# Gated linear attention and a feed-forward block: the same steps in another order on all engines, and the PSUM banks given out anew

## The chip, the cores and the metric

One core of one Trainium2 chip runs the whole kernel in one launch. The metric is the device time of one execution in microseconds (us). TensorE is PE in the profile, its weight loads PEld, VectorE is DVE, ScalarE ACT, GpSimd POOL, and SP is the engine that here issues all DMAs.

## The reference

Two blocks follow each other. The first is a gated linear recurrence for 4 batches, 8 heads, 768 tokens and 48 numbers a head:

```python
for t in range(S):
    state = alpha[:, :, t, :, None] * state + np.einsum('bhd,bhe->bhde', k[:, :, t], v[:, :, t])
    y[:, :, t] = np.einsum('bhd,bhde->bhe', q[:, :, t], state)
```

Its output, put together as x of 3072 tokens by 384, goes through a feed-forward block with 2048 inner features:

```python
h = x @ w_in
g = h * np.clip(h + 3.0, 0.0, 6.0) / 6.0
out = g @ w_out
```

[...]

## The kernel before

**Tiling.** Tokens are taken in 24 chunks j of 128, six to a batch, and the feed-forward block works on 12 groups g of two chunks. All matmuls are in 32-bit floats; each shows as two records in the trace.

**Steps.** The kernel is a list of some 1,790 words such as `M.6.5` or `m.15`. Each word names a step, and behind the dots stand its chunk or group, its part, and for steps that write PSUM or a shared buffer the number of the bank or buffer. The steps of the attention, for chunk j:

- `la`, `lk`, `lq`, `lv` load alpha, k, q, v (SP), `w` loads a slice of weights (SP, 768 KB). `d1`, `d2`, `dx` (ACT), `d3` (DVE) and `d4` (POOL) convert a slice.
- `ta`, `tk`, `tq` turn alpha, k and q: PE transposes into PSUM for the first six chunks (L282), DVE transposes after that. `ca` places alpha (ACT, later DVE); `r` and `p` are its two running products (DVE scans); `k` and `q` scale by them (DVE).
- `sc` are the scores of two halves of a chunk (PE, L346), `m` masks them into the tile A (DVE, four instructions of 0.41 us, L356), `qa` places q below them in A (ACT, L366).
- `kb` and `ck` turn k back by PE and ACT; from chunk 8 on `kt` (DVE), `kw` and `kr` (SP) do it through DRAM.
- `u` multiplies k by v (PE, L429), `sm` adds that to the state (DVE, L437 and L439), `st` decays the state (POOL, L409) and `sv` places it among the rows of v (ACT, L419).
- `ya` and `yb` multiply A by v and the placed state (PE, L455), `cy` copies the result out as x (ACT, L464).

The steps of the feed-forward block, for group g: group 0 and 1 use plain products `f`, `fa`, `fb` (PE, L478, L489) with `fr` (ACT) and `fg` (DVE) for the activation, and group 0's second product is `b`, `bo`, `so`. From group 2 on the first product is done by a scheme of 20 smaller products `M` of 8 matmul records each (L600): `x`, `y` and `xc` make the sums that it needs (DVE, L537, L541, L647), `n` copies a product out (ACT, L606), `o` combines (DVE), `e` and `h` are the activation (ACT L494, DVE L498). The second product is done from group 1 on by 7 products `P` of 16 records each (L703), with sums `s` (DVE, L647), copies `K` (ACT), sums `G` (DVE, L719; ACT for the last of four) and stores `O` (SP). `z.m.n` issues n filler matmuls into bank m, whose results nothing reads (L532).

**Order.** No scheduler reorders anything. `run` calls the steps of the list from left to right, each appends its instructions to the queues of its engines, and an engine goes through its queue in that order:

```python
for word in words.split():
    name, *at = word.split(".")
    steps[name](*(int(x) for x in at))
```

So the list fixes the order on every engine, and which step waits for which follows from the data and from the buffers. PSUM has eight banks: four (`banks`, number 0 to 3) for transposes, scores, `u` and `ya`, and four (`bank_m`) for the products of the feed-forward block and the fillers. A step that writes a bank waits until the last step that read it is done.

**Pads.** Chunks from 6 on are loaded in blocks into one of two buffers each for alpha, k and q. Six memsets (L257, POOL) fill the ends of such a buffer; they are part of `load_akq` for the first use of each buffer, that is in la, lk and lq of chunks 6 and 7.

Of the kernel before, what the change touches and what calls it, by code (L numbers as in the profile page):

```python
# [17 lines left out]
def kernel(  # L18
# [228 lines left out]

    def load_akq(name, j):
        src = rows({"a": alpha, "k": k, "q": q}[name], j)
        if j < FIRST:  # L250
            nc.sync.dma_start(out=ring[name, j % NR][:, :, 0:D],
                              in_=src.rearrange("h s d -> s h d"))
            return
        to = quads[name, j % NQ]
        if j < FIRST + NQ:
            for o in (BLK, 3 * BLK):
                nc.gpsimd.memset(to[o : o + BLK, :, V - 1, D - BLK : BLK], 1.0)  # L257
        to = to.rearrange("r p v d -> r p (v d)")
        t = src.rearrange("(p a) (u v) d -> a u p (v d)", a=2, v=V)
        for o in range(4):  # L260
            skip = BLK * (o % 2)
            nc.sync.dma_start(out=to[BLK * o : BLK * (o + 1), :, 0 : V * D - skip],
                              in_=t[o // 2, :, :, skip : V * D])
# [457 lines left out]
    def store2(g, i):  # L721
# [8 lines left out]
        "lq": lambda j: load_akq("q", j), "lv": load_v, "w": load_weight,  # L730
# [14 lines left out]
    def run(words):  # L745
        for word in words.split():
            name, *at = word.split(".")
            steps[name](*(int(x) for x in at))

    with tc.manual_schedule():  # L750
        run("""z.0.5 z.0.3 z.0.1 z.0.8 qa.0.0 w.0 d2.0 d3.0 la.0 ta.0.0 ca.0 r.0 lk.0 tk.0.1 k.0
               z.0.2 p.0 la.1 ta.1.2 lq.0 tq.0.3 ca.1 r.1 lk.1 lv.0.0 sv.0.0 d1.0 kb.0.0 ck.0 z.0.2
               u.0.2.1 sm.0.0 sv.0.1 q.0 qa.0.1 tk.1.0 k.1 p.1 z.0.2 sc.0.2.3 m.0 la.2 ta.2.0 ca.2
               dx.0 w.2 d2.2 kb.1.0 ck.1 lq.1 r.2 sm.0.1 st.1 tq.1.2 q.1 d3.2 z.0.3 d1.2 dx.2 lv.1.1
               u.1.3.1 sv.1.0 sm.1.0 p.2 sm.1.1 sc.1.0.2 m.1 ya.0.3 yb.0 cy.0 lq.2 w.1 d1.1 tq.2.1
               q.2 d4.2 lk.2 tk.2.3 k.2 fa.2.0 d4.0 st.2 sc.2.0.2 d2.1 d3.1 m.2 dx.1 d4.1 qa.1.1
               lk.3 la.3 ta.3.1 ca.3 la.4 fa.0.1 sv.1.1 w.3 r.3 ta.4.3 ca.4 r.4 tk.3.1 k.3 kb.2.0
               qa.1.0 d2.3 ya.1.2 yb.1 cy.1 fa.1.2 lq.3 ck.2 d1.3 p.3 d3.3 lv.2.2 u.2.3.2 sm.2.0
               d4.3 fb.2 tq.3.1 q.3 fb.1 qa.2.0 sm.2.1 sv.2.0 st.3 fr.0.2.0 fg.0.2 lk.4 tk.4.0
               sv.2.1 w.5 d2.5 k.4 d3.5 d1.5 qa.3.0 d4.5 qa.2.1 sc.3.1.3 m.3 w.6 d2.6 d1.6 d3.6 d4.6  # L760
               lv.3.0 lq.4 w.7 kb.3.2 fb.0 f.0.3.3 kb.4.0 ya.2.1 ck.3 u.3.3.2 sm.3.0 fr.0.3.1 fg.0.3
               fr.0.1.0 fg.0.1 qa.3.1 sv.3.0 sm.3.1 p.4 d2.7 sv.3.1 d1.7 d3.7 d4.7 f.0.5.0 fr.0.5.1
               fr.0.0.0 fg.0.5 fg.0.0 tq.4.3 ck.4 la.5 ta.5.2 f.0.6.3 ca.5 w.4 d2.4 ya.3.0 yb.3 cy.3
               fr.0.6.1 yb.2 cy.2 w.9 d2.9 q.4 qa.4.1 d1.4 d1.9 dx.4 la.6 w.8 d3.4 r.5 lk.5 w.10
               d3.9 p.5 ca.6 fg.0.6 d4.9 w.12 lq.5 lv.4.1 d2.8 d3.8 f.0.7.2 d1.8 st.4 d4.8 d4.4 w.11
               fr.0.7.0 fg.0.7 f.1.7.0 fr.1.7.1 fg.1.7 sc.4.0.2 m.4 f.1.1.1 fr.1.1.0 fg.1.1 f.1.3.3
               fr.1.3.1 d2.10 d1.10 tk.5.3 f.1.0.2 d2.12 d3.10 d4.10 w.13 fg.1.3 fr.1.0.0 fg.1.0 k.5
               d3.12 lq.6 f.1.6.0 f.1.2.1 u.4.1.0 sm.4.0 d1.12 d4.12 sv.4.0 qa.4.0 ya.4.2 fr.1.6.1
               fg.1.6 w.15 tq.5.3 fa.4.3 sv.4.1 d2.11 kb.5.1 d2.13 fr.1.2.0 f.1.4.2 fr.1.4.1 d1.11
               sm.4.1 q.5 r.6 d3.11 d3.13 fg.1.4 d4.11 lv.5.0 lk.6 tq.6 p.6 d2.15 d3.15 fg.1.2 d1.13  # L770
               d4.13 sc.5.0.3 yb.4 f.1.5.0 fr.1.5.1 fg.1.5 tk.6 m.5 b.1.0.2 fb.4 b.1.1 d1.15 d4.15
               st.5 y.5 w.14 la.7 lk.7 cy.4 d2.14 qa.5.1 ck.5 b.0.0.1 fr.0.4.0 d3.14 k.6 q.6 ca.7
               fg.0.4 d1.14 d4.14 x.0 y.1 y.10 b.0.1 y.0 y.2 u.5.2 P.1.0.0 K.1.0 qa.5.0 sv.5.0
               qa.6.1 P.1.1.3 b.0.2 b.1.2 kb.6.0 ya.5.3 y.6 s.1.0.0 sm.5.0 sv.5.1 G.1.0.0 tk.7
               s.1.1.1 s.1.2.3 x.1 yb.5 cy.5 b.1.3 sc.6.1.2 lv.6.2 ck.6 u.6.3.0 s.1.3.2 x.2 P.1.2
               b.0.3 K.1.1 y.7 s.1.4 s.1.5 y.11 y.3 r.7 xc.2.1 x.3 y.4 y.8 xc.2.3 k.7 xc.2.0 xc.2.4
               y.9 y.12 y.16 y.13 y.15 P.1.3.3 K.1.2 P.1.4 bo.1 P.1.5 xc.2.5 G.1.1.1 P.1.6 y.14 y.17
               y.19 xc.2.6 sm.6.0 G.1.2.2 y.20 M.2.0.2 lv.12.1 la.8 O.1.1 O.1.0 ca.8 y.18 y.21 y.23
               so.1 G.1.3.3 n.2.0.8 bo.0 lq.7 lv.7.0 O.1.2 m.6 xc.2.2 xc.2.10 xc.2.7 tq.7 r.8 p.7
               xc.2.8 sv.6.1 M.2.15.3 M.2.1 kb.7.3 n.2.1.9 M.2.16 M.2.2 n.2.2.10 M.2.7.0 n.2.7.11  # L780
               sm.6.1 xc.2.9 q.7 p.8 M.2.3 M.2.4 n.2.4.12 M.2.8 o.2.0.0 M.2.5 n.2.5.13 qa.7.0 sv.6.0
               st.7 lk.8 O.1.3 lq.8 lk.9 la.9 la.10 tk.8 tq.8 lq.10 lq.9 ya.6.1 yb.6 M.2.9 z.1.3
               M.2.18.1 o.2.1.0 e.2.1.1 M.2.10 cy.6 ck.7 sc.7.0.2 u.7.1.3 n.2.10.14 M.2.11 qa.7.1
               ca.9 la.11 y.22 M.2.6.2 h.2.1 q.8 m.7 e.2.0.0 h.2.0 n.2.11.15 qa.6.0 n.2.18.10 qa.8.1
               M.2.12 M.2.19 n.2.12.12 M.2.13 sm.7.0 sv.7.1 r.9 k.8 o.2.3.0 sv.7.0 ya.7.0 y.24
               o.2.5.0 n.2.13.12 o.2.2.0 yb.7 cy.7 sc.8.1.2 xc.3.1 o.2.2.1 e.2.2.1 xc.3.3 o.2.3.1
               M.2.14 xc.3.4 xc.3.0 xc.3.5 o.2.4.0 xc.3.7 xc.3.6 o.2.6.0 P.2.0.1 M.3.0.2 M.2.17
               h.2.2 o.2.6.1 e.2.3.0 h.2.3 o.2.7.0 K.2.0 n.3.0.12 M.3.1 n.3.1.9 e.2.5.1 M.3.7.0
               n.3.7.13 xc.3.8 o.2.7.1 xc.3.2 kt.8 e.2.6.0 h.2.6 tk.9 M.3.2 n.3.2.10 e.2.4.0 P.2.1.3
               h.2.4 h.2.5 s.2.0.14 e.2.7.0 G.2.0.1 h.2.7 M.3.3 M.3.4 n.3.4.8 k.9 s.2.1.11 M.3.8  # L790
               o.3.0.0 ca.10 kt.9 P.2.3.3 s.2.2.15 s.2.3.14 lv.8.2 kw.8 kr.8 lk.10 sm.7.1 xc.3.9
               M.3.5 n.3.5.11 K.2.2 e.3.0.1 xc.3.10 M.3.9 o.3.1.0 P.2.2 K.2.1 u.8.0.3 M.3.18.2 s.2.5
               M.3.10 n.3.10.14 n.3.18.15 e.3.1.0 s.2.4 P.2.4 tq.9 h.3.0 st.8 sv.8.0 M.3.11 n.3.11.8
               tk.10 p.9 sm.8.0 q.9 r.10 k.10 qa.9.0 qa.9.1 m.8 sm.8.1 h.3.1 M.3.19 o.3.5.0 kt.10
               P.2.5 G.2.2.0 st.9 M.3.12 sc.9.0.1 qa.8.0 n.3.12.10 o.3.3.0 kw.9 lv.9.0 kr.9 sv.8.1
               u.9.2.3 sm.9.0 sv.9.1 sv.9.0 G.2.1.2 sm.9.1 st.10 M.3.15.2 M.3.16 M.3.6.3 M.3.13 m.9
               o.3.4.0 o.3.6.0 tq.10 n.3.13.10 o.3.2.0 e.3.4.1 ya.8.2 yb.8 ya.9.3 yb.9 cy.9 M.3.14
               M.3.17 cy.8 xc.4.1 P.2.6 e.3.5.0 G.2.3.3 o.3.2.1 xc.4.3 h.3.4 xc.4.4 o.3.6.1 xc.4.5
               xc.4.0 xc.4.6 e.3.2.1 M.4.0.0 n.4.0.10 P.3.0.1 xc.4.7 o.3.7.0 p.10 h.3.5 o.3.3.1
               xc.4.8 M.4.7.3 M.4.1 xc.4.2 h.3.2 o.3.7.1 lk.11 O.2.2 tk.11 e.3.6.0 e.3.3.1 h.3.3  # L800
               P.3.1.2 e.3.7.1 n.4.1.13 M.4.2 K.3.0 ca.11 q.10 h.3.6 r.11 k.11 h.3.7 n.4.7.15
               lv.10.2 lv.11.0 kw.10 sc.10.0.1 kr.10 G.3.0.0 u.10.3.2 sm.10.0 qa.10.1 n.4.2.14 M.4.3
               M.4.4 M.4.8 s.3.0.9 xc.4.9 s.3.2.12 s.3.1.11 P.3.3.2 n.4.4.8 M.4.5 o.4.0.0 e.4.0.0
               sv.10.1 sm.10.1 xc.4.10 kt.11 O.2.0 O.2.3 lq.11 m.10 s.3.3.9 s.3.5 M.4.9 o.4.1.0
               P.3.2 sv.10.0 st.11 n.4.5.11 K.3.2 la.13 M.4.18.0 p.11 tq.11 lk.12 tk.12 K.3.1 M.4.10
               n.4.10.9 q.11 qa.10.0 n.4.18.12 e.4.1.1 la.12 s.3.4 ca.12 h.4.0 r.12 P.3.5 G.3.2.1
               h.4.1 M.4.11 P.3.4 n.4.11.8 M.4.12 n.4.12.14 qa.11.0 M.4.19 p.12 G.3.1.3 lq.12 kw.11
               O.2.1 tq.12 kr.11 u.11.3 sc.11.0.2 sv.11.0 O.3.1 lk.13 P.3.6 qa.11.1 M.4.6.2 G.3.3.2
               k.12 o.4.3.0 m.11 sm.11.0 sv.11.1 kt.12 M.4.13 n.4.13.14 q.12 o.4.3.1 e.4.3.0 o.4.2.0
               o.4.6.0 h.4.3 o.4.2.1 ya.10.1 ya.11.0 yb.10 yb.11 cy.11 cy.10 xc.5.1 ca.13 xc.5.3  # L810
               M.4.15.1 M.4.16 M.4.14 P.4.0.2 o.4.4.0 M.4.17 xc.5.4 o.4.5.0 xc.5.0 xc.5.5 M.5.0.0
# [121 lines left out]
```

## Time and profile before

| | |
|---|---|
| time, median of 3 runs | 533.5 us (533.48 to 533.62) |
| the profiled execution's own time | 533.84 us |
| its span in the profile | 531.8 us, so 2.0 us lie around it |
| TensorE's granted clock over the span | 1.00 |
| busy: PE, DVE, ACT, POOL | 522.2, 477.0, 257.4, 50.4 us |
| M products (L600), 1,600 records | 82.8 + 52.5 + 42.0 + 31.8 us in four groups |
| P products (L703), 1,232 records | 121.7 + 91.5 us in two groups |
| filler matmuls (L532), 58 records | 10.2 us |
| pads (L257), 12 memsets on POOL | 0.9 + 0.8 + 0.6 us |

The span runs from the first to the last instruction or transfer of the execution. Busy time is the time in which at least one instruction of an engine was running; PE's matmuls overlap each other, so the sum of the groups' means is larger than the busy time. In the view of 40 slices one slice is 13.3 us and a digit is the busy share in tenths. "A <- B" in a view of waits reads: the step A stood idle until B was done.

### The profile page before, as it was taken

To read this page: it belongs to the slowest core of one execution; us is meant where nothing else is said; L and a number is where in the kernel's file an instruction comes from. 1 tells how busy PE (TensorE), PEld (TensorE's weight loads), DVE (VectorE), ACT (ScalarE), POOL (GpSimd) and SP (SyncE) were. 2 spreads that over 40 slices of the span, in tenths; PEclk is the share of its full clock that TensorE was granted. 3 is DMA by queue.
4 is the path that set the end of the run, shared out by engine and by line. 5 is a ranking of instruction groups with operands and counts; after the bars stand their busy time and mean duration, and the time that the engine had idled before them with its cause. 6 is when DMAs were issued, how large, how long until landed. Compare 5 with 4: busy or idle time off the path is not lost.

```text
span 531.8 us, 15143 instructions
## 1 busy us (share of the span) xinstructions
PE 522.2 (98%) x6306; PEld 496.9 (93%) x6306; DVE 477.0 (90%) x849; ACT 257.4 (48%) x503; POOL 50.4 (9%) x71
## 2 busy tenths in 40 slices
PE   7799999999999999999999999999999999999997
PEld 7698886789999999999999999999999999999997
DVE  6999989999999999999999999999999899496382
ACT  3889865212653553553544444642634544553340
POOL 5333425100000000000000000000000000000000
PEclk9999999999999999999999999999999999999999
DMA  9998887006615156254345356055364052100001
GB/s 173 218 254 247 211 231 156 18 2 149 155 31 118 30 125 139 49 137 100 89 107 118 90 123 143 18 134 111 92 138 105 10 110 44 44 2 2 15 16 37
DMA packets 124100, 54.40 MB, mean 102 GB/s; under 512 B 83328, under 2 KB 116864, under 8 KB 124032
## 3 DMA queue, kind: packets, MB, share of 16 engines
q1 hardware_dynamic: 124032, 53.44, 44.0%
q8 instruction: 49, 0.80, 0.7%
q14 instruction: 19, 0.16, 0.1%
HBM read 44.50 MB, written 8.91 MB: 100 GB/s over the span
## 4 chain that ended last, share of the span: by engine, by line
PE 81%; DVE 9%; ACT 3%; DMA 3%; POOL 2%; issue 1%; SPq 0%; DVEq 0%; POOLq 0%; ACTq 0%
PE m_ps L703 34%; PE m_ps L600 34%; PE m_ps L478 4%; PE t_ps L455 3%; PE t_ps L346 2%; PE t_ps L429 2%; DMA v<-in_v_dram 1%; DMA raw<-in_moe_w_out_dram 1%; DVE rings L647 1%; DVE R L309 1%; DVE raw L537 1%; ACT raw L186 1%; DVE g_sb L647 1%; ACT raw L191 1%; DVE w L537 1%
## 5 line engine op out<-in xcount | busy, mean ns | idle before, releaser
L606 ACT COPY g_sb<-m_ps 128x512 f32<-128x512 f32 x110 | 63.6, 584 | 123.7 <-PE m_ps L600 104.3
L703 PE MATMUL m_ps<-w,g_sb 128*128 128x192 f32 x704 | 121.7, 327 | 0.0
L703 PEld LDWEIGHTS m_ps<-w,g_sb 128*128 128x128 f32 x704 | 113.7, 190 | 0.4
L703 PE MATMUL m_ps<-rings,g_sb 128*128 128x192 f32 x528 | 91.5, 326 | 0.0
L703 PEld LDWEIGHTS m_ps<-rings,g_sb 128*128 128x128 f32 x528 | 85.4, 190 | 0.1
L600 PE MATMUL m_ps<-xc,w 128*128 128x128 f32 x640 | 82.8, 277 | 0.4 <-DVE w L541 0.4
L600 PEld LDWEIGHTS m_ps<-xc,w 128*128 128x128 f32 x640 | 77.5, 192 | 1.7 <-issue 0.6
L494 ACT ACTIVATE r<-g_sb,half 128x512 f32<-128x512 f32 x80 | 56.8, 722 | 33.1 <-DVE g_sb L541 12.1
L498 DVE SCALAR_TENSOR_TENSOR g_sb<-r,g_sb 128x512 f32<-128x512 f32 x80 | 53.7, 683 | 4.3 <-ACT r L494 3.9
L600 PE MATMUL m_ps<-xT,raw 128*128 128x128 f32 x400 | 52.5, 277 | 0.0
L600 PEld LDWEIGHTS m_ps<-xT,raw 128*128 128x128 f32 x400 | 48.6, 192 | 0.6
L409 POOL TENSOR_TENSOR st<-sm,R 128x192 f32<-128x192 f32 x20 | 12.9, 643 | 352.2 <-DVE sm L439 305.5
L647 DVE TENSOR_TENSOR g_sb<-g_sb 128x512 f32<-128x512 f32 (+1 forms) x55 | 41.9, 792 | 0.2
L600 PE MATMUL m_ps<-xT,w 128*128 128x128 f32 x320 | 42.0, 276 | 0.0
L600 PEld LDWEIGHTS m_ps<-xT,w 128*128 128x128 f32 x320 | 39.3, 192 | 0.1
L366 ACT COPY A<-q 48x256 f32<-48x256 f32 x88 | 35.6, 404 | 5.0 <-DVE q L332 3.8
L356 DVE TENSOR_TENSOR A<-t_ps,mask 64x256 f32<-64x256 f32 x96 | 36.0, 413 | 0.4
L478 PE MATMUL m_ps<-xT,w 128*128 128x256 f32 x144 | 32.8, 382 | 0.1
L600 PE MATMUL m_ps<-xc,raw 128*128 128x128 f32 x240 | 31.8, 276 | 0.0
L309 DVE TENSOR_TENSOR_SCAN R<-t,ones 128x516 f32<-128x516 f32 x24 | 29.6, 1235 | 1.0 <-ACT t L300 0.9
L478 PEld LDWEIGHTS m_ps<-xT,w 128*128 128x128 f32 x144 | 26.7, 190 | 3.8 <-POOL w L217 0.2
L600 PEld LDWEIGHTS m_ps<-xc,raw 128*128 128x128 f32 x240 | 29.6, 192 | 0.1
(104 smaller groups left out, 725.8 us busy)
## 6 DMA issues: line engine op xcount, KB each, us to landing
raw<-in_moe_w_out_dram SPq DMA_DIRECT2D x8, 768.0 KB, 5.3
raw<-in_moe_w_in_dram SPq DMA_DIRECT2D x6, 768.0 KB, 6.6
v<-in_v_dram SPq DMA_DIRECT2D x48, 96.0 KB, 3.1
out_dram<-oh SPq DMA_DIRECT2D x44, 96.0 KB, 1.7
far<-kq SPq DMA_DIRECT2D x64, 64.0 KB, 2.2
kb<-far SPq DMA_DIRECT2D x64, 64.0 KB, 2.1
aq<-in_alpha_dram SPq DMA_DIRECT2D x36, 96.0 KB, 2.7
qq<-in_q_dram SPq DMA_DIRECT2D x36, 96.0 KB, 2.5
```

The costliest lines, as they stand in the source:

```text
L309: nc.vector.tensor_tensor_scan(out=reverse(R, n - 1, n), data0=reverse(ax, n, n), data1=reverse(ones, n, n), initial=0.0, op0=ALU.mult, op ...
L356: nc.vector.tensor_tensor(out=to[:, a], in0=sc[a][half], in1=mask[half, half].unsqueeze(1).to_broadcast([HB, NP, HB]), op=ALU.mult)
L366: nc.scalar.copy(out=to[:, a], in_=Q_t[j][64 * a : 64 * a + D, :, half])
L409: nc.gpsimd.tensor_tensor(out=st, in0=sm, in1=R_t[j][:, :, 0:1].to_broadcast([C, NP, D]), op=ALU.mult)
L455: nc.tensor.matmul(y_of(j, (i + 1) // 2, p)[:, HB * b : HB * b + HB], vb[:, p, e : e + 32], A_t[j][:, b, 2 * p + a], start=(b == 0 and i = ...
L478: nc.tensor.matmul(h[:, f], w1[:, kk, o : o + C], xT_t[g][:, kk], start=(kk == 0), stop=(kk == KT - 1))
L494: nc.scalar.activation(out=to, in_=h, func=AF.Relu, bias=half, scale=1.0 / 6.0)
L498: nc.vector.scalar_tensor_tensor(out=to, in0=r, scalar=1.0, in1=h, op0=ALU.min, op1=ALU.mult)
L600: nc.tensor.matmul(acc[g][i][:, f * C : (f + 1) * C], spots[w][:, f * C : (f + 1) * C], x_of(g, x), start=(first and f == 0), stop=last, s ...
L606: nc.scalar.copy(out=slots[z], in_=acc[g][i])
L647: nc.vector.tensor_tensor(out=out, in0=in0, in1=in1, op=ALU.subtract)
L703: nc.tensor.matmul(to[g], a, rhs[:, f], start=(first and f == 0), stop=(last and f == HF - 1), skip_group_check=True)
```

## The change

**A new step.** The memsets leave `load_akq` and become a step of their own, `pd`, one word for each of the two sets of buffers:

```diff
+    def pad(r):
+        for name in "akq":
+            for o in (BLK, 3 * BLK):
+                nc.gpsimd.memset(quads[name, r][o : o + BLK, :, V - 1, D - BLK : BLK], 1.0)
+
     def load_akq(name, j):
...
         to = quads[name, j % NQ]
-        if j < FIRST + NQ:
-            for o in (BLK, 3 * BLK):
-                nc.gpsimd.memset(to[o : o + BLK, :, V - 1, D - BLK : BLK], 1.0)
...
-        "lq": lambda j: load_akq("q", j), "lv": load_v, "w": load_weight,
+        "lq": lambda j: load_akq("q", j), "lv": load_v, "pd": pad, "w": load_weight,
```

**A new list.** All words are put into another order, so every engine's queue changes. Apart from the bank numbers the words are the same, but for `pd.0` and `pd.1`, which come in, and four words `qa.0.0`, `qa.6.0`, `qa.12.0` and `qa.18.0`, which issued nothing and go. The number of filler matmuls stays 29, of which 13 instead of 17 stand ahead of the first transpose. The start of the list:

```diff
-        run("""z.0.5 z.0.3 z.0.1 z.0.8 qa.0.0 w.0 d2.0 d3.0 la.0 ta.0.0 ca.0 r.0 lk.0 tk.0.1 k.0
-               z.0.2 p.0 la.1 ta.1.2 lq.0 tq.0.3 ca.1 r.1 lk.1 lv.0.0 sv.0.0 d1.0 kb.0.0 ck.0 z.0.2
-               u.0.2.1 sm.0.0 sv.0.1 q.0 qa.0.1 tk.1.0 k.1 p.1 z.0.2 sc.0.2.3 m.0 la.2 ta.2.0 ca.2
-               dx.0 w.2 d2.2 kb.1.0 ck.1 lq.1 r.2 sm.0.1 st.1 tq.1.2 q.1 d3.2 z.0.3 d1.2 dx.2 lv.1.1
...
+        run("""w.0 z.0.5 la.0 lq.0 lk.0 z.1.8 la.1 d2.0 lv.0.0 d1.0 d3.0 pd.0 ta.0.0 z.1.1 lk.1
+               ca.0 sv.0.0 tq.0.1 dx.0 r.0 la.2 pd.1 z.1.3 w.2 tk.0.0 p.0 z.1.2 lq.1 ta.1.2 k.0
+               d4.0 z.1.2 ca.1 lv.1.1 q.0 kb.0.3 z.1.2 ck.0 sc.0.1.2 lq.2 r.1 qa.0.1 u.0.3.0 z.1.3
+               sm.0.0 z.0.3 m.0 sv.0.1 ya.0.3 w.1 yb.0 sm.0.1 d2.2 p.1 la.3 tk.1.0 ta.2.2 cy.0 lk.2
```

The stretch around chunk 15:

```diff
-               n.6.18.10 K.5.1 P.5.5 G.5.2.3 r.16 k.16 e.6.0.0 h.6.0 h.6.1 o.6.6.0 M.6.19 n.6.10.15
-               o.6.5.0 M.6.11 tq.16 P.5.4 qa.15.1 sc.15.1.2 m.15 u.15.0.3 n.6.11.12 sv.14.0 sv.14.1
-               st.15 sv.15.0 sm.15.0 M.6.12 n.6.12.14 o.6.3.0 sm.15.1 kt.16 G.5.1.1 p.16 M.6.15.3
-               M.6.16 M.6.13 n.6.13.14 o.6.4.0 ca.17 o.6.2.0 ya.15.1 ya.14.2 yb.14 sv.15.1 yb.15
...
+               P.5.5 K.5.1 sm.14.0 lq.18 ca.16 sv.14.1 sm.14.1 r.16 la.18 M.6.9 st.15 u.15.2.0 k.16
+               sv.15.0 sc.15.1.3 o.6.1.0 P.5.4 sm.15.0 e.6.1.1 p.16 sv.15.1 sm.15.1 kt.16 st.16
+               M.6.10 kw.16 q.16 G.5.1.1 m.15 M.6.5 n.6.10.15 ya.15.0 n.6.5.11 yb.15 r.17 lk.18
```

**Banks.** 151 words write another bank than before, among them 35 `M`, 23 `u`, 22 `P`, 20 `sc` and 14 `ya`; `ya.15.1` above, for example, becomes `ya.15.0`, and `sc.15.1.2` becomes `sc.15.1.3`. Lines behind the new function stand two lower in the changed kernel's profile.

## The prediction

> **What bounds the kernel now.** I read the busy table and the 40 slices first, then the stretches by stage, then the waits of TensorE (PE) and of VectorE (DVE), then the timeline around one late hand-over. The page first:
>
> ```profile
> PE 522.2 (98%) x6306; PEld 496.9 (93%) x6306; DVE 477.0 (90%) x849; ACT 257.4 (48%) x503; POOL 50.4 (9%) x71
> PE   7799999999999999999999999999999999999997
> DVE  6999989999999999999999999999999899496382
> ACT  3889865212653553553544444642634544553340
> DMA  9998887006615156254345356055364052100001
> ```
>
> PE is full from the third slice on, but DVE is nearly as full until slice 31 of 40, and the DMA rings are full in the first seven. So an order that delays DVE a little can delay PE. By stretches (busy us of each engine, then clock, DMA share, GB/s):
>
> ```profile
> 0.00:13.30 13.30, 10.58 (x64) 9.72 (x64) 8.62 (x17) 4.76 (x6) 7.12 (x20) 1.00 1.12 173
> 13.30:26.60 13.30, 9.99 (x243) 8.30 (x246) 12.89 (x26) 11.72 (x16) 4.28 (x3) 1.00 1.08 218
> 40.00:60.00 20.00, 19.92 (x276) 16.99 (x275) 19.56 (x31) 19.59 (x34) 7.51 (x7) 1.00 0.77 232
> 60.00:80.00 20.00, 20.00 (x222) 17.33 (x221) 18.38 (x32) 13.56 (x22) 7.30 (x8) 1.00 0.86 225
> 200.00:250.00 50.00, 50.00 (x595) 49.37 (x586) 47.52 (x87) 22.09 (x46) 0.51 (x1) 1.00 0.45 102
> 450.00:500.00 50.00, 50.00 (x526) 49.50 (x525) 30.80 (x60) 20.19 (x41) 0.00 (x0) 1.00 0.07 16
> ```
>
> PE loses 6 us in the first 26.6 us and almost nothing later; DVE has 2.5 us to spare in 200 to 250 us and plenty after 450. The waits after 32 us, of PE (first line, the only one) and of DVE from 130 to 400 us (the three largest):
>
> ```profile
> PE m_ps L600 <- DVE w L541: 0.4, 1, 0.4
> DVE g_sb L537 <- PE m_ps L600: 2.1, 3, 1.2
> DVE g_sb L498 <- ACT r L494: 1.3, 3, 0.6
> DVE xc L537 <- ACT xT L464: 1.0, 1, 1.0
> ```
>
> In the middle it is DVE that waits for PE, never the other way round after 128 us. One place shows the spare time, the mask of chunk 15 (m.15, L356) in front of its attention product (ya.15, L455):
>
> ```profile
> 301.82 1.95 PE L600 MATMUL m_ps<-xT,raw 128*128 128x128 f32 x16
> 301.87 0.77 DVE L356 TENSOR_TENSOR A<-t_ps,mask 64x256 f32<-64x256 f32 x2
> 303.60 1.06 PE L600 MATMUL m_ps<-xc,raw 128*128 128x128 f32 x8
> ```
>
> The last two of m.15's four mask instructions end at 302.64, ya.15 starts on PE at 304.59: 1.95 us spare.
>
> **How I count.** For each engine I add what lies ahead of a step in its list, start to start: PE 0.893 us for an M (8 records of 0.112), 2.60 for a P (16 of 0.163), about 0.4 to 0.5 for a transpose, score or attention word, 0.1 more at a change from big to small products; DVE the mean of the row less the 82 ns by which its instructions overlap, and 117 ns more where one waits for the instruction right before it. A step's lag is its start in the trace less that sum. PE's lag is 1.5 us at its first filler, 12.0 at 32 us, 14.5 at 147 us, 16.2 at ya.15, 18.0 at the last product (526.2). DVE's is 8.8 at m.2 (27.9 us), 14.3 at 144 us, 19.7 at m.15; from 144 us on it grows by waiting for PE, as the rows above show.
>
> **The change, part by part.**
>
> *Work.* The same instructions run, but for four words that issued nothing. PE's sum is 510.8 us before and 510.3 after (43 instead of 46 changes from big to small products): **-0.5**. DVE's is 468 in both. Waits on the instruction just before go from 82 to 84 on DVE, 0.2 us, taken at nothing. The last store's chain (P.11.6, an eviction on ACT, a store) is the same: 0.
>
> *Pads.* Twelve memsets (L257, 0.9 + 0.8 + 0.6 = 2.3 us in all on POOL) leave the loads of chunks 6 and 7 and run early as pd.0 and pd.1, around the state copy sv.0.0 and ahead of POOL's first weight conversion d4.0. POOL is at 7.12 of 13.3 us there, waiting for d3. Price for d4.0 between 0 and 2.3 us; it reaches only fa.0's weights, which come after the transposes, and I take 0. Behind the old place (47 to 84 us) nothing waited for POOL: no gain.
>
> *Front.* 13 filler matmuls (z, two records each) instead of 17 stand ahead of the first transpose ta.0. In the trace filler records start 213 ns apart until 6.96 us and 111 ns apart from then on; 26 records from 1.47 end at about 7.0, just behind alpha's landing (6.93), so ta.0 can start at about 7.1 instead of 7.97: -0.9. A rule of the Trainium skill speaks against this edit: "TensorE: Matmul & The Clock Gate", Part 1, has the clock open only after some 3.4 us of sustained work, in a window that runs freely, so the number of slow matmuls differs from run to run; were it to open later, ta.0 would run slow. By the two spacings ta.0's eight records would then cost 8 x 0.10 = 0.8 us more, and the sum below would be 0.8 higher at worst. This trace opened the clock 5.5 us after the first filler, and I take the same point. Of the 0.9 little is left on DVE: the new SP order brings q's first chunk before k's, so lk.0 and la.1 land about 1.2 us later (loads of this size land that far apart here: la.0 6.93, lk.0 8.16, lq.0, two later, 10.55), and lk.2 about 0.8 later. Adding up to m.2 I get an end at 29.2 to 29.6 against 29.42: DVE is where it was. PE gains more. In the old order DVE's sum up to q and ACT's copy for ya.1 was 3.9 us longer than PE's sum ahead of ya.1; in the new one the worst such place of the first 30 us (m.2 ahead of ta.4) is 1.9. PE's lag at 32 us comes out 1.5 to 2 lower: about **10 to 10.5**.
>
> *Middle.* Here the new order spends what the front gives. Covers are PE's sum ahead of the consumer less DVE's sum up to the end of the producer; PE's lag has to be at least DVE's lag less the cover.
>
> m.7 to sc.8: 132.8 - 129.2 = +3.5 before; 129.6 - 131.2 = -1.6 after.
> m.11 to ya.11: 210.0 - 207.0 = +2.9; 204.8 - 207.8 = -3.1.
> m.15 to ya.15: 288.4 - 282.8 = +5.5; 281.7 - 285.8 = -4.2.
> G.7.1 to P.7.6: 368.0 - 356.9 = +11.0; 360.4 - 364.1 = -3.8.
>
> (0.1 us of hand-over is in each.) The new order puts 3 us more of DVE's work ahead of m.15 and takes 7 us of PE's work away from before ya.15. If DVE is at m.15 with the lag of 14.3 that it had at 144 us, and loses nothing more, m.15 ends at 285.8 + 14.3 = 300.1 and ya.15 starts at 300.2, with a PE lag of 18.5, against 16.2 before: **+2.3**. DVE's lag at that place is bounded by 12.3 (8.8 as at m.2, and 3.5 of the 5.5 us that it lost from 28 to 144 us) and by 17 (14.3 and half of the 5.4 us of waits of 144 to 301 us): PE lag 16.5 to 21.2, that is +0.3 to +5.0. I take 14.3, since the new front leaves m.2 where it was, ACT is as full in 40 to 60 us (19.59 of 20 us), and DVE's waits for PE mostly go when PE is the late one. DVE's longest wait for ACT at 40 to 50 us, by the sums 1.1 us in the old order (d3.8) and 1.9 in the new (fg.0.7), is inside these bounds.
>
> *Banks.* 151 words write another PSUM bank. Each step's wait for the last reader of its bank is in the covers above: m.7 to sc.8 is such a wait (the scores of chunk 8 take the bank that m.7 reads). Without the renaming that place would be bound 0.6 us less tightly (m.7 to ya.7, -1.0).
>
> *End.* After G.8.1 to P.8.6 (-1.3) the covers grow fast, to over 30 us for s.11.0 to P.11.3 in both orders. The 1.8 us of lag that PE still gains behind ya.15 I leave as they are.
>
> *Sum*: -0.5 + 2.3 = **+1.8** on the profiled 533.84 us (span 531.8 and 2.0 around it): 535.6. That execution is 0.3 above the median of 533.5, so the forecast is **535.3**. About 0.2%, 1.1 us, can be told from no change.
>
> **Rivals.**
>
> *PE keeps the front's gain.* If DVE's lag at m.15 is under 12.5, ya.15 is no later than before, net of the 0.5. With the 8.8 of m.2 and 3 us more, every cover above is met with a PE lag of 16.0, and the old growth behind it stays: 533.5 - 0.5 - 0.2 = 532.8; with the small losses of PE in the old middle (2.6 us of lag from 147 to 382 us) partly not repeated, as low as 531.5. For it: 1.1 of DVE's 1.6 idle us at 60 to 80 us were one wait for PE's state product (s, L439), which a PE that is 2 us earlier would remove. Against it: DVE's list is full in between, and four covers have to hold, not one.
>
> *DVE and PE hold each other up by turns.* The new order has places where DVE waits for PE close to those where PE waits for DVE: o.2.0 needs a DVE lag of at least PE's less 0.8, then ya.9, ya.11 and ya.15 need PE at DVE's plus 2.0, 3.1 and 4.2. The turns add 0.5 to 1 us each; three or four of them give 537 to 538.5. For it: all these numbers are within 1 us of each other from 120 to 400 us. Against it: each sum may be off by 0.5 us either way.
>
> *k's way through DRAM becomes the bound.* From chunk 8 on k goes out and back by DMA (kt to u, some 8.3 us). u.16 has 10.1 us for it by the sums, 10.8 before. It decides if the queue of SP holds a kr back by over 1.8 us; each us beyond is a us on PE: 534 to 537.
>
> **How the numbers follow.** DVE binds the middle once: 0.42, around 535.3 (533.9 to 536.5). By turns: 0.15. DRAM: 0.05. PE keeps the gain: 0.28, most of it below 532.4. A wash, in which front and middle cancel (532.4 to 534.6): 0.10. With the edges of the first and the fourth case that is faster 0.27, same 0.16, slower 0.57. The range runs from 531.6 to 538.4; the likeliest case's own range is 533.9 to 536.5.
>
> **What would show it.** Right: PE waits for m (L356, two lines lower in the changed kernel) at ya.11 or ya.15, or for G or o of 200 to 390 us, by 3 us or more in all; DVE's idle time from 130 to 400 us falls from 10 to under 6 us; ta.0 at 7.1, and PE's lag at 32 us down by 1.5 to 2. Wrong: PE has no wait over 0.5 us after 60 us while DVE still idles, or u, sc and ya wait for a DMA.

## The result, and the profile after

The changed kernel takes 550.1 us against 533.6 for the old one. The ratio is 1.031 (95% interval 1.026 to 1.036): slower by 16.5 us, where 1.8 was forecast, and outside the range. One run of the changed kernel took 1369 us and one of the run named both 1882 us; the measured times here are averages of the other, undisturbed runs (548.5, 549.5 and 552.3 us for the changed kernel), while the expectations below speak of medians of all runs, 550.9 and 542.0. The profiled execution of the changed kernel is the longest of its three: it took 552.27 us, its span is 550.5. The page of the changed kernel, the same rows as were shown of the old one:

```profile
PE 529.0 (96%) x6306; PEld 499.8 (91%) x6306; DVE 479.4 (87%) x849; ACT 261.8 (48%) x503; POOL 53.2 (10%) x71
PE   8789989899999999999999989989999999999997
DVE  7899889999999999999999979998999966575391
...
DMA  9999796032304633552455453463143230000000
```

PE's row has 8s where it was full before, in slices 3, 6, 8, 24 and 27. The work is the same to 0.5 us, so the 18.7 us of span are time in which PE stood or ran slow. The stretches say where (busy us of each engine, clock, DMA share, GB/s):

```profile
40.00:60.00 20.00, 19.68 (x303) 16.59 (x303) 17.05 (x28) 17.84 (x33) 5.46 (x5) 1.00 0.96 239
60.00:80.00 20.00, 17.49 (x140) 14.23 (x138) 17.66 (x27) 11.80 (x18) 8.63 (x6) 1.00 0.90 230
200.00:250.00 50.00, 50.00 (x639) 49.22 (x638) 48.59 (x88) 23.88 (x48) 0.51 (x1) 1.00 0.45 104
```

In 40 to 60 us the DMA share went from 0.77 to 0.96, and DVE and ACT, which were full there, lost 2.5 and 1.8 us. PE pays in the next stretch. The waits of ACT from 36 to 110 us name what came late, the weights, which ACT's steps begin to turn from 64-bit into 32-bit floats. The old kernel has one such wait (first line), the changed one six (the other two lines):

```profile
ACT w L196 <- DMA raw<-in_moe_w_out_dram: 3.6, 1, 3.6
ACT raw L186 <- DMA raw<-in_moe_w_out_dram: 5.7, 3, 2.2
ACT w L196 <- DMA raw<-in_moe_w_out_dram: 3.4, 3, 2.1
```

PE's waits behind 32 us, the six largest, where there had been one of 0.4 us:

```profile
PE m_ps L480 <- DVE g_sb L500: 1.9, 2, 1.3
PE t_ps L431 <- DMA v<-in_v_dram: 1.7, 2, 1.3
PE m_ps L705 <- ACT oh L718: 1.5, 1, 1.5
PE t_ps L457 <- issue: 1.3, 1, 1.3
PE m_ps L705 <- DVE g_sb L500: 1.1, 1, 1.1
PE m_ps L705 <- DVE oh L721: 1.1, 3, 0.6
```

VectorE is named for the most, 5.8 of the 12.0 us of the whole view, but no single hand-over stands out: products wait for an activation (L500), the state update for v's load, a copy into a store buffer (oh) for that buffer's store, a product for an output sum on DVE (L721), and one stop has no releaser at all. The chain that ended last shows the queue of SP in it, which it was not before (the old kernel's chain first):

```profile
PE 81%; DVE 9%; ACT 3%; DMA 3%; POOL 2%; issue 1%; SPq 0%; DVEq 0%; POOLq 0%; ACTq 0%
PE 56%; DVE 27%; DMA 6%; SPq 5%; issue 4%; ACT 3%; DVEq 0%; ACTq 0%
```

PE's lag, counted as in the prediction (start less the sum of the work ahead; the end of the work in the last column), for the old kernel, the changed one, and four of the experiments below (the row of need_order is the changed kernel's less the difference of their starts at the same products):

| PE's work done, us | 40 | 60 | 80 | 100 | 200 | 280 | 300 | 400 | 420 | 505 |
|---|---|---|---|---|---|---|---|---|---|---|
| old | 12.5 | 12.7 | 12.8 | 13.3 | 15.4 | 16.1 | 16.3 | 17.3 | 17.6 | 18.0 |
| changed | 12.3 | 15.5 | 18.3 | 19.4 | 23.6 | 26.2 | 30.4 | 34.4 | 36.2 | 37.2 |
| need_order | 12.7 | 14.6 | 15.8 | 16.1 | 19.8 | 22.7 | 23.5 | 25.8 | 26.0 | 26.9 |
| both | 11.6 | 13.5 | 13.5 | 14.6 | 18.3 | 20.7 | 21.4 | 23.6 | 25.4 | 26.4 |
| front_old2 | 12.7 | 12.9 | 13.7 | 14.1 | 16.2 | 19.0 | 20.2 | 22.4 | 23.6 | 24.6 |
| both_light_dve | 12.7 | 14.6 | 14.6 | 15.7 | 17.7 | 19.5 | 20.1 | 21.3 | 23.3 | 24.0 |

The changed kernel gains 7 us of lag between 40 and 100 (old: 0.8), 7 more up to 280 (2.8), 4.2 between 280 and 300, and 7 to the end (1.7). Its first part is not all of the list's making: need_order has the same instructions in the same order on every engine up to 130 us, and its execution is 3.3 us earlier at 100. There ACT's waits for weights are 3.4 us instead of 9.1:

```profile
ACT w L196 <- DMA raw<-in_moe_w_out_dram: 2.1, 1, 2.1
ACT raw L186 <- DMA raw<-in_moe_w_out_dram: 1.3, 1, 1.3
```

So 3.3 us of the lag shown for the changed kernel belong to this one execution.

### The profile page after: what moved, and what is told of

Same layout as the page of the kernel before. It is cut to its first block, busy times and chain, and to the rows that moved or that the text cites. A ratio compares the mean times of both kernels' runs of the same rounds, so it can differ in the third digit from the quotient of the medians.

```text
span 550.5 us, 15098 instructions
## 1 busy us (share of the span) xinstructions
PE 529.0 (96%) x6306; PEld 499.8 (91%) x6306; DVE 479.4 (87%) x849; ACT 261.8 (48%) x503; POOL 53.2 (10%) x71
## 4 chain that ended last, share of the span: by engine, by line
PE 56%; DVE 27%; DMA 6%; SPq 5%; issue 4%; ACT 3%; DVEq 0%; ACTq 0%
PE m_ps L705 25%; PE m_ps L602 21%; PE t_ps L457 3%; DVE g_sb L649 3%; SPq L264 2%; DMA v<-in_v_dram 2%; DVE g_sb L500 2%; DVE A L358 2%; PE m_ps L480 2%; DVE g_sb L539 2%; DVE q L288 2%; DVE k L288 2%; DMA kq<-in_k_dram 2%; DVE R L311 1%; PE t_ps L348 1%
## 5 line engine op out<-in xcount | busy, mean ns | idle before, releaser
L602 PE MATMUL m_ps<-xc,w 128*128 128x128 f32 x640 | 84.2, 280 | 0.4 <-DVE g_sb L543 0.3
L602 PEld LDWEIGHTS m_ps<-xc,w 128*128 128x128 f32 x640 | 78.7, 194 | 1.9 <-DVE g_sb L543 0.5
L500 DVE SCALAR_TENSOR_TENSOR g_sb<-r,g_sb 128x512 f32<-128x512 f32 x80 | 54.3, 689 | 7.2 <-ACT r L496 6.9
L602 PEld LDWEIGHTS m_ps<-xT,raw 128*128 128x128 f32 x400 | 49.3, 194 | 0.7
L411 POOL TENSOR_TENSOR st<-sm,R 128x192 f32<-128x192 f32 x20 | 15.5, 776 | 348.1 <-DVE sm L441 323.5
L358 DVE TENSOR_TENSOR A<-t_ps,mask 64x256 f32<-64x256 f32 x96 | 36.2, 415 | 1.9 <-PE t_ps L348 1.4
L539 DVE TENSOR_TENSOR g_sb<-g_sb 128x512 f32<-128x512 f32 x40 | 26.8, 684 | 9.9 <-ACT g_sb L608 9.6
```

Source lines behind the costliest of these rows:

```text
L358: nc.vector.tensor_tensor(out=to[:, a], in0=sc[a][half], in1=mask[half, half].unsqueeze(1).to_broadcast([HB, NP, HB]), op=ALU.mult)
L500: nc.vector.scalar_tensor_tensor(out=to, in0=r, scalar=1.0, in1=h, op0=ALU.min, op1=ALU.mult)
L539: eng.tensor_tensor(out=out, in0=in0, in1=in1, op=ALU.add if s1 > 0 else ALU.subtract)
L602: nc.tensor.matmul(acc[g][i][:, f * C : (f + 1) * C], spots[w][:, f * C : (f + 1) * C], x_of(g, x), start=(first and f == 0), stop=last, s ...
```

## The experiments

Theory 1 is throughout the one that the traces suggest, theory 2 its rival; each run's text says which they are.

**1. SP's queue alone, first the loads ahead of 95 us.** The changed list issues the loads of chunks 5 to 8 between the weight slices. In the old one SP stood waiting for a free weight buffer instead (23.6 us of waits of w for d4 from 36 to 110 us, 6.2 in the changed kernel), so each slice went out the moment its buffer was free, with little beside it. In the changed kernel two things happen. Slices beside chunk loads land more slowly: w.8, issued at 49.3 us, had landed in 5.7 us, and now goes out at 43.5 and takes 10.5; ACT waits 0.9 us for it. And slices go out later, because chunk loads stand ahead of them in SP's queue: w.10, w.12, w.11 and w.13 are issued 7 to 11 us later than in the old kernel and take 4.7 to 7.9 us to land (4.5 to 7.0 before); ACT waits 7.8 us for these four. SP's order in weights_first, the other engines' queues kept except for two memsets on POOL:

```diff
- w.7 la.5 w.4 la.6 lk.5 w.8 lq.5 w.9 lv.4.1 lv.6.2 lk.7 w.10 lq.6 lk.6 la.8 w.12 lq.7 la.7 w.11
- lv.5.0 w.13 lv.12.1 w.15 w.14 lq.8 lk.8
+ w.7 la.5 w.4 w.8 lv.4.1 w.9 la.6 w.10 lk.5 w.12 lq.5 w.11 lq.6 w.13 lk.6 w.15 lv.5.0 w.14 la.7
+ lq.7 lk.7 lv.6.2 lv.12.1 la.8 lq.8 lk.8
```

> The changed kernel, with SP's queue alone reordered between w.7 and lk.8: the weight slices go ahead of the loads of chunks 5 to 8, as in the old list (and POOL's two memsets sv.6.0 and sv.12.0 behind d4.14). Theory 1 (early chunk loads take bandwidth from the weights): w.8 lands about 5 us earlier, PE's lag at 107 us falls from 19 to 13 or 14 us, and the time from 550.9 to 543 to 546 us. Theory 2 (the new list of VectorE is the loss, whenever the loads come): 549 to 552 us.

Measured: 547.1 us (ratio to the old kernel 1.025, 1.023 to 1.028), 3.0 less, between the two theories; the intervals of the two ratios overlap, so this gain is not clear of the noise. ACT's waits for weights went from 9.1 us to 0.3, and w.8, issued at 44.0, landed in 5.3 us. PE's lag at 100 us of work fell from 19.4 to 16.1, but that is where need_order has it too, without this edit.

**2. SP's queue behind chunk 8.** In the changed list an lk that has to wait for the k buffer (free when kw has landed) stands ahead of the kr that reads k back, and v's load behind both. SP's own view of the changed kernel around chunk 16 (kw L398, lk L264, kr L406, lv L274):

```profile
306.06 2.58 SPq L398 DMA_DIRECT2D far<-kq  x4
308.73 3.31 SPq L264 DMA_DIRECT2D kq<-in_k_dram  x4
312.10 1.81 SPq L406 DMA_DIRECT2D kb<-far  x4
314.01 3.45 SPq L274 DMA_DIRECT2D v<-in_v_dram  x4
```

v.16 landed at 318.6, and u.16, which PE had reached at 316.7, waited for it. The edit at that place, and the like at some 35 words in all:

```diff
- kw.16 lk.18 kr.16 lv.16.0 lv.17.1 O.5.1
+ kw.16 O.5.1 lv.16.0 kr.16 lv.17.1 lk.18
```

> The changed kernel, with SP's queue alone reordered behind lk.8: kr goes ahead of the lk that waits for the same buffer, and lv, kw and O go by when they are needed. Theory 1 (SP's queue hands k, v and free store buffers over too late from 180 to 440 us): PE's waits at u.9, u.12, u.16 and at the product behind the late store go, 4 to 8 us less than 550.9. Theory 2 (VectorE's list): at most 1 us less.

Measured: 543.5 us (1.019, 1.016 to 1.021), 6.6 less: theory 1. The waits for v and for a store buffer are gone. Of the 10.2 us by which this profile is shorter, 3.3 lie ahead of the edit, as said; 6.9 lie behind it.

**3. Both orders of SP's queue.**

> Both reorderings of SP's queue in the changed kernel; all other engines as changed. Theory 1: 534 to 539 us, of which some 2 us over the old kernel are the covers of m.11 and m.15 that the prediction counted. Theory 2: 548 to 552 us.

Measured: 541.8 us (1.016, 1.014 to 1.018), 8.3 less than the changed kernel and 1.7 less than need_order, of which the last is not clear of the noise. The result lies between the theories, nearer to 1: SP's order is half of the loss, and 8.2 us stay, over four times what was forecast.

**4. The same early loads in the old kernel.**

```diff
- w.4 w.9 la.6 w.8 lk.5 w.10 w.12 lq.5 lv.4.1 w.11 w.13 lq.6 w.15 lv.5.0 lk.6 w.14 la.7 lk.7 lv.6.2
- lv.12.1 la.8
+ w.4 la.6 lk.5 w.9 lq.5 w.8 lv.4.1 lv.6.2 lk.7 w.10 lq.6 lk.6 la.8 w.12 la.7 w.11 lv.5.0 w.13
+ lv.12.1 w.15 w.14
```

> The old kernel, with SP's queue alone changed between w.4 and la.8: the loads of chunks 5 to 8 are pulled ahead of the weights w.8 to w.14, as in the changed kernel. Theory 1: weights land 3 to 5 us later, 536 to 541 us. Theory 2: 533 to 534.5 us, as before.

Measured: 541.5 us (1.015, 1.013 to 1.017): 7.9 us for the loads of some chunks moved ahead, a little over theory 1's range. The computing of the other engines is in its old order; in the old kernel the pads belong to the loads, so POOL's memsets move with them. ACT's waits for weights from 36 to 110 us went from 3.6 to 11.9 us (first line). The second line is SP's own, in the same stretch, and the old kernel has no such wait:

```profile
ACT w L196 <- DMA raw<-in_moe_w_out_dram: 11.9, 3, 5.7
SPq L272 <- PE t_ps L455: 12.4, 4, 6.4
```

This is a load of v that waits for its buffer, which an attention product still reads, while the weights behind it wait in the queue. SP stood at lv.12.1 from 73.1 to 77.2 and from 77.9 to 84.3 us; w.15, the next word, went out at 85.0 instead of 73.1, and ACT waited 5.4 us for it. Another 5.7 us were for w.12, issued at 67.2 instead of 59.6 behind three chunk loads, and landed in 5.4 us. So 11.1 of ACT's 11.9 us come from the places of the loads in SP's queue, and not from the bandwidth that they share with a slice in flight.

**5. Which part of the new list costs the other 8.2 us?** Two mixed lists, cut at 95 us and at 36 us. First the old list up to ck.5, then the new one with SP's queue as in both. In the first form of this (front_old) three filler matmuls wrote into the bank of group 0's product fa.4 before it was read; front_old2 has them removed.

> The old list up to ck.5 (some 95 us, weights ahead of the chunk loads; two banks renamed), then the new list with SP's queue by need, as in the run named both. Theory 1 (covers in the middle cost 3 us to 300 us and 3 more to 430 us): 539 to 541 us. Theory 2 (the new list loses in the first 100 us only): 533.5 to 536 us.

> As front_old (old list up to ck.5, then the new list with SP's queue by need), without the three fillers that overwrote a product there. Theory 1 (what is left of the loss lies behind 100 us): 539.5 to 540.5 us. Theory 2: 533.5 to 536 us.

Measured: 540.5 and, without the fillers, 539.0 us (1.010, 1.009 to 1.011), just under theory 1's range. The new order ahead of 95 us costs 2.8 us (541.8 - 539.0), the one behind it 5.4 (539.0 - 533.6). Then the new list in front and the old one behind; in the first form a score of chunk 3 overwrote ya.2 before it was copied, in the second the cut lies ahead of ya.2:

> The new list up to fg.0.2 (some 40 us; pads early, fa.0 and fa.2 with exchanged banks), then the old list for all that is left. Theory 1 (the front is worth up to 1 us to PE, the loss lies behind): 532.5 to 534 us. Theory 2 (the new front already puts VectorE and the loads back): 535 us or more.

> The new list up to fr.0.2.0 (some 36 us), then the old list; the cut lies ahead of ya.2, whose bank a score overwrote in front_new. Theory 1 (PE's gain of the front, 0.9 us of lag at 33 us in the run named both, is kept by the old middle): 532.5 to 533.3 us. Theory 2 (the old order behind it waits for ACT and for VectorE as before, and takes the gain back): 533.5 to 536 us.

Measured: 535.7, and 534.3 (1.0011, 1.0002 to 1.0020). The gain that the new front brings PE is not kept.

**6. Does VectorE hold the new middle?** Half of the four mask instructions of each chunk left out, in both kernels:

```diff
-            for a in range(2):
+            for a in range(1 if j >= FIRST else 2):
                 nc.vector.tensor_tensor(
                     out=to[:, a], in0=sc[a][half],
```

> The kernel of the run named both (changed order, SP's queue mended), with half of the mask instructions (L358) left out from chunk 6 on: 18 x 2 x 0.41 = 15 us of VectorE's work less, spread over 100 to 460 us; the scores' other half is not masked into A. Theory 1 (VectorE's sum ahead of m, o, G and s sets PE's place in the middle): 542.0 falls to 535 to 538 us, and DVE's waits for PE come back. Theory 2 (what is left is PE's own, its instruction fetch or its banks): 541 to 542 us.

> The old kernel with the same half of the mask instructions (L356) left out from chunk 6 on. Theory 1: PE sets the pace there, so the 15 us that VectorE is spared are worth at most 1 us: 532.5 to 533.6 us. Theory 2: the same; a fall of more than 2 us would say that VectorE bound the old kernel too.

Measured: 540.1 us (1.012, 1.011 to 1.014), 1.7 less than both, which is at the edge of the noise, and 533.4 for the old kernel (0.9996, 0.9986 to 1.0005). 15 us of VectorE's work gave back less than 2. So a larger cut: also the sums o and the products h on half of their columns,

```diff
-            add(nc.vector, at, acc[g][h], sh, at, sa)
+            add(nc.vector, at[:, 0:256], acc[g][h][:, 0:256], sh, at[:, 0:256], sa)
```

> The kernel of the run named both, with VectorE made light from group 2 on: half of the mask instructions left out (from chunk 6 on), and the sums o (L539, L541, L543 on g_sb, 81.5 us) and the products h (L500, 54.3 us) done on half of their columns, so that half of the hidden values are left as they were: some 75 us of VectorE's 479 less. Theory 1 (VectorE's place in the new list is what is left behind 100 us): 536 to 538 us. Theory 2 (it is ACT, TensorE's fetch or PSUM banks): 539.5 us or more.

> The old kernel with the same work left out on VectorE. Both theories: TensorE sets the pace there, so 532 to 533.5 us; some of that is the shorter chain of o, h and the last products at the end.

Measured: 538.4 us (1.009, 1.007 to 1.011), 3.4 less than both, between the two theories; the old kernel 533.3 (0.9994, 0.9984 to 1.0004). VectorE does hold the new list and not the old one, but for less than half of the 8.2 us. DVE's busy time in the span fell from 478.9 to 420.8 us:

```profile
PE 523.7 (97%) x6306; PEld 496.9 (92%) x6306; DVE 420.8 (78%) x813; ACT 260.7 (49%) x503; POOL 52.8 (10%) x71
```

What PE still waits for there is in the front, but for an issue stop of 1.5 us at 422 us and two waits for output sums (L721) of 0.7 in all.

**7. The stop without a releaser.** In both it is in the middle of an attention word, yb.20, of which three records come late; nothing that the profile shows held them. PE's timeline there:

```profile
423.80 1.75 PE L457 MATMUL t_ps<-A,v 128*32 128x64 f32 x105
426.85 0.30 PE L457 MATMUL t_ps<-A,v 128*32 128x64 f32 x3 [1.29 <-issue]
```

The page counts 49 packets, 0.80 MB, of kind instruction on queue 8 in the old kernel: 16 KB each, and 12,612 records of PE and PEld (twice 6306) make 257 to a packet. In both they start 10 us apart in the median, but around this stop at 424.5 and 428.1 us, and around a stop at 190 us at 187.4 and 191.2 (a third such pair, at 480.6 and 484.0, has no stop). Four attention words in a row use up one packet (4 x 64 records); where PE does not stop they take 1.9 us. Two ways of breaking those bursts:

```diff
- ya.21.3 yb.21 ya.20.0 yb.20 M.9.17 P.8.5
+ ya.21.3 yb.21 P.8.5 ya.20.0 yb.20 M.9.17
```

> The kernel of the run named both, with two words moved on TensorE: P.2.6 goes between the attention words of chunks 9 and 8, P.8.5 between those of chunks 21 and 20, so that four attention words (256 short records in 3.8 us) no longer stand in a row at 185 and 424 us. Theory 1 (TensorE runs out of fetched instructions there: waits put down to issue of 0.8 and 1.3 us, between two fetches on queue 8 that lie only 3.6 to 3.8 us apart): both waits go, 542.0 falls by 1.5 to 2.5 us. Theory 2 (these are late releases by VectorE): no change, 541.5 to 542.5 us.

Measured: 545.0 us (1.020, 1.019 to 1.022), slower than both. The stops went, and in their place stand waits for what the later attention words hand on (PE from 180 to 450 us, both_split):

```profile
PE m_ps L705 <- DVE oh L721: 2.7, 3, 1.5
PE m_ps L602 <- DVE g_sb L543: 1.1, 1, 1.1
```

With a short product in place of the long one (M.9.16, moved from ahead of ya.21 to behind yb.21, and M.3.16 likewise):

> The kernel of the run named both, with M.3.16 moved between the attention words of chunks 9 and 8 and M.9.16 between those of chunks 21 and 20 (0.9 us each, both already due), in place of the 2.6 us words of both_split. Theory 1 (TensorE's instruction fetch): the waits marked issue at 190 and 425 us go, and nothing is late in their place: 539.5 to 541 us against 542.0. Theory 2 (the stop is a late release, which the profile does not see): 541.5 to 542.5 us.

> The same, with half of the mask instructions (L358) left out from chunk 6 on, as in both_less_dve (540.2 us). Theory 1: the stop of 2.0 us at 423 us goes: 538 to 539 us. Theory 2: 540 us.

Measured: 542.9 and 540.2 us, no better than without the move. PE from 180 to 430 us, first in both, then in both_split2:

```profile
PE t_ps L457 <- issue: 1.3, 1, 1.3
PE m_ps L705 <- DVE oh L721: 0.9, 2, 0.6
PE m_ps L705 <- issue: 0.8, 1, 0.8
```

```profile
PE t_ps L457 <- DVE A L358: 0.9, 1, 0.9
PE m_ps L705 <- DVE oh L721: 0.7, 2, 0.4
PE t_ps L457 <- DVE s L441: 0.5, 1, 0.5
PE t_ps L457 <- issue: 0.3, 1, 0.3
```

The stop is cured (0.3 left), and a mask and a state sum are late by as much. That the fetch is what stops PE fits the cure, and need_order, which has the same words on PE, its packets there 4.5 us apart and no stop at that place. Against it, pairs under 3.9 us apart with no stop are in several profiles (both_split: 190.3 and 193.9). It was not measured by itself.

**8. The old kernel's only late start.** PE waits 0.4 us at M.2.1 for y.23, which stands behind ca.8 on DVE; ca.8 goes behind y.23.

> The old kernel with one word moved on VectorE: ca.8 (L286, 1.09 us) goes behind y.23, for which TensorE waits 0.4 us (0.58 late in its own row) at M.2.1, the only place behind 32 us. Theory 1 (TensorE sets the pace there, so its one late start is worth its size): 532.9 to 533.2 us. Theory 2: 533.5 us, because VectorE's next step is late instead.

Measured: 533.8 us (1.0002, 0.9993 to 1.0010): no change. The late start is gone from its place, and M.2.8, a few products on, starts 0.44 late. No run is faster than the old kernel by more than the noise, not even those that leave work out.

No run has the new order with the old PSUM banks, or the old order with the new ones, so what the banks do by themselves is open.

## Why the prediction was wrong

- **The step that failed is DVE's lag at m.15**, "14.3, and loses nothing more", with bounds of 12.3 and 17. In the profile of the changed kernel it was 22.5. At m.2 it was near the forecast (9.2 for 8.8), at m.5, 107 us, it was 19.7 instead of 12.7, and flat from there to 150 us. These 7 us came in between 50 and 107 us, where ACT waits for weights. 3.3 of them are this execution's own (need_order, the same up to there, has 16.4 at m.5); with the weights first and kr by need, DVE's lag was 14.9 at m.5 and 17.1 at m.15, and PE's 20.7, about at the upper ends of 17 and 21.2.
- **What was left out is SP's queue past the front.** The prediction walked the loads to m.2 and stopped. It counted ACT as full in 40 to 60 us, and did not ask whether its weights would still be there: la.6, lk.5 to lk.7, lq.5 and lv.6 were moved ahead of slices that had landed with 1.7 to 5 us to spare (w.9, w.8, w.10). This term is 8.3 us together with the next.
- **The rival of k's way through DRAM** was given 0.05 and 534 to 537 us. Its point, a kr held back by 1.8 us, was reached at chunk 16 (kw's data had landed at 310.3, kr began at 312.1), but v's load behind it was the one that PE waited for. The need-order run puts 6.6 us on the queue there, with late stores.
- **The mechanism that was forecast is there.** In the old kernel ya.11 started 3.8 us after the last mask that it needs, in six profiles of the new order with all masks 0.04 us after it, and in both_less_dve and both_light_dve, with half of them left out, 0.37. At m.15 the hand-over was counted from its last mask to ya.15; it is yb.15, 0.47 us behind ya.15, that needs that mask, so the cover of -4.2 is in effect -3.7. PE's lag less DVE's is 3.7 in the changed kernel (26.2 - 22.5) and 3.6 in both. What DVE's lag would be, on which it all rests, was wrong.
- **The signs** that the prediction named are mixed. PE's recorded waits for m, G and o from 200 to 390 us are 0.6 us in the changed kernel and 0.9 in both, where 3 were asked for: a PE that is already late does not stand at these places. DVE's idle time from 130 to 400 us is 8.7 us in the changed kernel and 3.5 in both (9.4 in the old), where under 6 was asked for. A sign of being wrong came: u.16 waits 1.7 us for a DMA.
- **The direction** was right, and partly by luck: half of the loss is a term that the prediction did not have.
- **"The 1.8 us of lag that PE still gains behind ya.15 I leave as they are"** was the second wrong size: 11.0 in the changed kernel (26.2 to 37.2 at the last product), 5.7 in both. Part of it may be the turns by which DVE and PE hold each other up (a rival at 0.15), part the stop at 425 us; no run takes them apart.
- **The front**: ta.0 started at 7.0 for 7.1. m.2 ended at 30.1 us for 29.2 to 29.6, in both at 29.4. PE's lag of 10 to 10.5 at 32 us was not reached: 12.0 in the changed kernel at 36.6 us (ya.2), 11.3 in both.
- **The rule on the clock** that was weighed there did not bear on the result: ta.0's records start 0.11 us apart, as at full clock. The Trainium skill ("TensorE: Matmul & The Clock Gate", Part 1) has PE slow down again after some 3.4 us of idleness; here the clock fell after less (below).

The account of the 16.5 us by runs: 8.3 SP's order (changed to both), 2.8 the new list ahead of 95 us (both to front_old2), 5.4 behind it, of which some 3 go when VectorE is made light (3.4 less the 0.4 that the old kernel gains). Some 2 us are not settled: a stop of 1.3 us in the waits at 425 us lies there, but curing it brought nothing, and the banks were not tried.

## What to carry to other kernels

An order is priced on every queue to its end: a load that is moved ahead holds up what stands behind it in the queue, by the time to issue it and by its own wait for a buffer, and slows what is loaded beside it. So ask which transfer with little to spare now stands behind it, and put the urgent one first. Compare profiles of the same instructions before a difference is put down to an edit: here 3.3 us of it were there without one. A cover says how far the consumer must lag behind the producer; what it costs hangs on the lag that the producer will have, not on the one that it had. Where two engines are both full, removing one wait shows the next, so the sum of the rows is no forecast of what a cure brings; run it.

## What the runs showed of the hardware

- Waiting in the queue of SP is not a loss in itself: the old kernel waits 23.6 us there for weight buffers, and its weight slices of 768 KB issued from 46 us on land in 4.4 to 7.0 us; in the changed kernel, with chunk loads beside them, w.8, w.9 and w.4 took 8.8 to 10.5.
- TensorE stopped with no releaser for 0.5 to 1.7 us in bursts of short matmuls, in several profiles at 190 and 425 us, where two 16 KB instruction packets lie 3.5 to 4.2 us apart. Other such pairs have no stop, so the fetch of instructions is an inference.
- After two waits of 1.34 and 0.38 us around 316 to 319 us the granted clock of the stretch 320 to 340 us is 0.92, and the products M.6.17 and M.6.14 took 0.8 us more each than their rows; the profile of both, without those waits, has 1.00. In need_order the clock of 20 to 25 us is 0.66, behind waits of 0.17 and 1.51 us. But weights_first has waits of 1.1 and 0.7 us for v between 311 and 315 us and a clock of 1.00 from 310 to 330, so how much waiting brings the clock down is open.
- Such a fall of the clock shows in the time. Of front_new2's twelve runs the five with a mean clock of 0.996 or 0.997 took 534.7 to 536.1 us, the seven with 0.999 or 1.00 took 533.4 to 533.9. The changed kernel's three averaged runs have 0.994 to 0.997, those of both 1.00, 0.997 and 1.00, so a part of the 8.3 us between them may be slower clock.
